# A conformer block on one core: the plan derived anew, with block order and PSUM banks searched together

## The chip, the cores and the metric

The kernel runs on one core of a Trainium2 chip. The metric is device time in microseconds (us) of one execution. The core has five instruction streams that run side by side and wait for each other by semaphores: PE (TensorE, the matmuls), ACT (ScalarE, activations), DVE (VectorE, elementwise work), POOL (GpSimd, small elementwise work) and SP (SyncE, which here only issues DMAs).

## The reference

Two sequences of 4000 tokens with 144 channels go through one conformer block. Cut to what is computed:

```
x = x + 0.5 * (silu(ln(x) @ w_ff1a) @ w_ff1b)          # 144 -> 576 -> 144
q, k, v = split(ln(x) @ w_qkv), 4 heads of 36
x = x + softmax(q k^T * 36**-0.5) v @ w_o               # 4000 x 4000 per head
a, b = split(ln(x) @ w_pw1);  h = a * sigmoid(b)
x = x + silu(depthwise_conv5(h)) @ w_pw2
x = x + 0.5 * (silu(ln(x) @ w_ff2a) @ w_ff2b)
return ln(x)
```

Inputs and output are bf16, x and the output have the shape (2, 4000, 144).

## The kernel before

**Tiling.** The 8000 tokens are 16 chunks of 500, eight for each sequence; a chunk is four blocks of 125 tokens, which lie on the partitions. X stays in SBUF. A chunk passes three stages. `pre` (L1267) is the first feed-forward (`ff1`, L1200) and then `pre2` (L1241), which makes the queries, keys and values. Attention runs over 18 phases: a phase is one chunk of queries against keys in tiles of 64 keys, 63 tiles in all (62 of 64 keys, one of 32). The first two chunks of queries have two phases each, since the last keys of the first sequence come late; their sums are saved between. `post1` (L1341) and `post2` (L1465) do the output projection, the gated convolution and the second feed-forward.

**An attention tile.** PE makes scores for 64 keys and 500 queries of four heads (two PSUM banks, four matmuls QK), ACT or DVE makes the exponentials, PE multiplies them with the values (four matmuls PV into banks 6 and 7). On ACT one instruction of 1000 columns does a tile (`emit_exp`, L1631). On DVE a tile takes five instructions (`dve_tile`, L1645): two that bring 500 columns each from PSUM to an integer, two that take the bits apart, and one product. Such a tile leaves two factors, so it has eight PV matmuls instead of four.

**Turning a chunk round.** Before a matmul of the feed-forward or of q, k, v the normalized chunk must have its channels on the partitions. For the very first chunk and at the end PE does it. Everywhere else it goes through DRAM (`blocks`, L885): DVE transposes blocks of 32 x 32, SP issues four DMAs that write the rows to a scratch tensor (`rows<-XN` or `rows<-AN`), waits until they have landed, and issues two DMAs that read them back: `XT<-rows` for the feed-forwards, the output projection and the gate, `XTQ<-rows` for q, k and v. SP works its list in order: a read that waits for its writes holds up all that stand behind it. Ahead of the DVE transpose stands the layer norm (`ln`, L953): statistics on DVE, then a power and four scalings on POOL.

**What sets the order.** While the program is built, `Rec.op` (L148) notes every instruction with the tiles that it reads and writes and a cost in us; `Rec.LAT`, `SEM` and `SWITCH` are added for latencies. Generators (`Thread`, `Sched`, L378 to L450) say what could go on, and `pick_any` (L1785) takes the next by estimated times and by the numbers in `POLICY` (L496), which hold for stretches of 21 attention tiles. In `blocks` a DMA of SP costs 0.36 us, a write lands 2.0 us and a read 2.4 us after it:

```
SP_COST = 0.36
W_LAT = 2.0
T_LAT = 2.4
```

All of this makes a first order, cut into blocks (what one step of a generator issued on one engine). `reorder` (L208) then moves the blocks of each engine by the table `ORDER` (L35): one letter for a block, P for one that stays, letters behind or ahead of it for one that moves by so many places. `finish` (L242) works out which semaphores each instruction must wait for, and `replay` (L286) issues the lists; nothing is decided on the chip. Since all is issued by line 296, every record of the profile has that line, and the names of the tiles tell what it is.

**PSUM.** Banks 0 to 5 are handed out by `Banks` (L326) as the first order is made. A tile keeps the bank that it was given there, whatever `reorder` does with its block, and the waits on a bank are those of the first order: an instruction that writes a bank waits for the readers of the tile that had it before.

**At the start and the end** there are dummy matmuls on the identity (`warm`, L781): 50 at first, and more wherever the first order shows a gap on PE before the first exponential and after the last.

Of the kernel before, what the change touches and what calls it, by code (L numbers as in the profile page):

```python
# [22 lines left out]
NB = 4  # L23
# [13 lines left out]
        "PPPPPPQOPPPPPQOPPPSPPMPPPQRNQNPPPQOROQNXOOOPPMOOhPggNPRILJLNRJOKLJNLMMMMMMPPPPPRPNPPPPQOPPRPNPPPPPPP"  # L37
        "PPPQOPPPQOUUNNNNNPPPWWNNOOLNNPPPQSPMOQOPQQNPP^PNOZZMOZKKLLLLMKRTMMPNPRPNPPPPQOPPPPPPPPPPPPPPQOPPPPPP"
        "SOOOWQVMRWSJKKQJNPPROOPPPPPPQOPPPPPPPPPPPQQNPPPPPQOPPPQOPQOPPPQOQOPRPNPSOOQNPQOPPSOOQNPPROOPQOPPQOPP"
        "WOPUMUVMMJLRSLSLUULTOUJUJTNTHSKRSTLTVFUKLSLSLLQNPPRRRMMQQNPPPPPPQOPQOPPQOQOQQQMPPSOOOPSPNOPPPQQNPPPQ"  # L40
        "QNPPQOPPQOPPQOPPRPNPPPPPPPPPQOPPPPPPQOPPPRRNNPPQOPPQQNQOPRRNQQQKPPPPPPPPPPRORPMPQOPPPPPQOQOPPQOQOQOP"
        "PPPPPQOPPPPPPPQQNPPPPPPPQOROOPPPPPQOPPPPPPPPQOQQNPPPPPPPPPPPPPPPPPSQRMMQQNPPPPQOPPQRNQQMPQOPPQOPPQOP"
        "PPPPPPPPPPPPPPPPPPPPPPPPPPPPPPPPQOQRRMQMPQQNROOQOPPQQQMPPPPQOPPPPPPPPQOPPPPPPPPPQOPQOPPPPQQNPPPPPPPP"
        "PPPPQOPPPPPPPPPPPPPPPPPPPPPPPPPQOTOQNSMPTMPNORPNPROQRMQQMPPPPQUNOSNNSMOQNPROOPRPQMSPNOPPSOPNQOPRPNPQ"
        "OQOPPQOTOPNOPPPPPQOPPPPPPPPPPPPPQOPPPQQNPPPSOOOPPPPQOQQNPQQRMQRRRKMPSQNNSOOQQMPPQQNQOPPPPSOOOPPQQQMP"
        "PPPPPPPQQNPPPQOPPQOPRPQMPPPPPQOPPTQNNOPPPPPPQQNPPSOOOPPQOPPPPPPPPPPPPPQOPRPNPQOPPQQNROOPQQNPPPPPPPPP"
        "PQOPPPPPPPPQOPPPPPPPPPPPPPQOPPQOPPPPPPPPPPPPPPPPPPPPPPPPSSOMQMPPQQNPQRNRNOQQQMPSOOOPPQQQQLPQOQOROOTP"
        "NOOPPPPPQOPPPPQOPPQOPQOPPPPPPPPPPQOPPPPQOPPQQNQOURNNNQNPPPPPRPQMPPPPPPPPRORNQQQLPSOOOQQQQQKPPQQNQOPP"
        "PPPPPQOPPPPPPPSOOOPPQOQOPPROOPQQN]OOOOOPNXNORLQLLQNPPROORRSNLVNWNNNNNOQNQOPQOPPPPPPPPPPPPPPPQOPPPPQO"
        "PROOPQQNPPPQQNPPPQOPPPPPPPQOPPPPQOPPPQQNPQOQOQOPPPQQNPPPQRNQNPPQOPPPPPPPPPPPPPROOPPPPPPPPPPPPQOPPPRO"  # L50
        "QNPQQNPQOROOPQOQQQQQKROOSOOQNPQOPPPPQOPQOPPPPPPPPPPPPPPQOPPPQOPPPPPPPQOPPQOPPWOOOOOOOQRPMPROOPPPPPPP"
        "PPQOQQNPQQQMQQQMQTPMRNNRPNPRPNPPPPPQQNRRRNLQQNPPQOPQOPSPNOTOOROMPPPRPNPQOSSSMMMQQNPPPQQNQOQQNQQQMQOP"
        "PPQQNPRRNNPPQRNOPPPPPQOPPSOOOPQQNRRNNPPPQQQQLPPPQOPPQQNROOTOOPNSOOOPPRTQMPQKPQQNPPRSQMMPPPPPPPPPPPPP"
        "PQOPPPPPPPPPPQOROOSOOQNQOPQQNPPPPPPQOPPPPQOPQOPPPPPTOPSMPQLPQOQOPQOPPQRPMSOPNSQNNPPPPPPPPPPPPPPQOPPP"
        "PPRRNNPQQNRPQRLOQRPMRRNNPRPNPRPNPQOPQRNOWOOPNOPNPPPSSNOMPQQNPPPPPQOPQOPPQOPQTNSNOSLOQNQOPPQOPPPQOPRP"
        "QMPPPQOPPPPQOPQOPQOPQOQOPRPNPPPPPQQQRLOPRPNPPPPPPPPPPPPPPPQOQOQOSOOOPPQOPPPPPQOQOPPPPPPPPPPQQQMPPPPP"
        "PPPPPQOPPPROQNPPPPPQOPPSOOOPSORNNPSOPNPPPPPPQOPPPPPPPPPPPPPPPPPPPPPPPPPPSOOOPPPPPPPPPPPPQOQOPPPPPQQV"
        "MRTQLRKQQIPPRPNQOPPPPQOQQNPPPROQNPPQOPPPPQQQMROOPQOPRSSMMQMQOQRRMQMQQNSQOTLPNQNQOQOQOPPQQNTQSMMQRLVN"
        "OOPNQNPPQQNPPPQQNROOQOPROOQOPQOPPPQOPPPPQOQOPPPPQOPQOPPPPPPPPQOPPPQOQOQQQMPPPUPNOOQQMRPNTOOOOPPQQNPS"
        "OOOQQNPPPPPPPQOPROTNOOOPQOPPPPPPPQOPPQOPPQOPQOPPQOPQQNQORRNNPPPQOPPQOPQOQOPPPPQSPMQNPPPPROQNPPPPPPPP"  # L60
        "PPPPPPPPPPQORRSMMOPSORNRMQNPPPQRNOPQRNOQOPPQOPPPPQOPPPPPPPROOPQOPQOPSOPQMPQQNPPPPPPPQOPPPPPPPPPPPPQO"
        "PPPQOPPPROQNROOPPPPPPPPQOPPPROOPPPPQOPQOPPQOPPPPPPQOPQOPPQOPPPQOPQOPQOQOPPPPPPPPPQOPPPPPPPPPPPQOPPPP"
        "PPPPPQQNPPQOPQQNPPPQOPPQOPPQOSOORROLPSPNQNPPPPPPPPPPPQOPPQOPPQOPPPPPPPPPPQOPPRPNQOPPPRPNVOOOOOOROQNP"
        "QQQQLPQORPNPQRNOROOPRORNOTOQRTQSSIISQKNPRPNPPPQOPPPPPPPTTOSLMMQQSMORPMQOTOPNQNPROOQOQOQQNQRRMQQRRJQM"
        "PPROQRPLQQQMQQNQSNPNPQQQQRKOTQXRLLPPKOOQOPSTNNNOPPPQOPQOPPRTNVMQNPPJQO"
    ),
    "act": (
        "PPPPPPPPPPPPPPQOROOPPQOPPQOQOPPPROOSOOOPQOQOPQOQOPPPPPPPPPPPPRPNPPPPPPPPROOPQOPPPPPPPPPPPPPPPPPPQOPP"
        "QOPPPPPPPPPPPPPPPPPPPPPPPPPPPPPPPPPPPPPPPPPPPPPPPPPPROOQOPPPPPPPPPPPPPPPPPPPPPPPPPPPPPPPPPPPPPPPPPPP"
        "PPPPPPPPPPPPPPPPPPPPPPPPPPPPPPPPPPPPPPPPPPPPPPPQOPPPPPPPPPPPPPPPPPPPPPPPPPPPPPPPPPPPPPPPPPPPPPPPPPPP"  # L70
        "PPPPPPPPPPPPPPPPPPPPPPPPPPPPPPPPPPPPPPPPPPPPPPPPPPPPPPPPPPPPPPQOPPPPPPPPPPPPPPPPPPPPPPQOPPPPPPPPPPPP"
        "PPPPPPPPPPPPPPPPQOPPPQOPQOPPPPPPPPPPPPPPPPPPPPPPPPPPPPPPPQQNPQOPPPPPPPPPPPPPPSOOOROOPPPPPPPPPPPPPPPP"
        "PPPPPPPPPPPPPPPPPPPPPPPPPPPPPPPPPPPPQOQOPPQOPPPPPPPPPPPPPPPPPPPPPPPPPPPPPPPPPPPPPPPQOPPPPPPPPPPPPPPP"
        "PPPPPPPPPPPPPPPPPPPPPPPPSOOOPQOPPPPPQOPPPPPPPPPPPPPPPPPPPPPPPPPPPPPPPPPPPQOPPPPPPPPPPPPPPPPPPPPPPPPP"
        "PPPPPPPPPPPPPPPPPPPPPPPPPPPPPPPPPPPPPPPPPPPPPPPPQOPPPPPPPPPPPPPPPPQOPPPPPQOPPPPPPPPPPPPPPPPPPPPPPPPP"
        "PPPPPQOPPPPPPPPPPPPPPPPPPPPQOPPPPPPQOQOPPPPPPPPQOPPPPPPPPPPPPPPPPPPPPROOPQOPPPPPPPPPPPPPPPPPPPPPPPPP"
        "PPPPPQOPPPPPPPPPPPPPPPPPPPPPPPPPQOPPPQOPPPPPPPPPPPPPPPPPPPPPPPPPPPPPPPPPPPPPPPPPPPPPPPPPPPPPPPQOPPPP"
        "PPPPPPPPPPPPPPPPPPQOPPPPPPPPPPPPPPPPPPPPPPPPPPPPPPPPPPPPPPPSOOOPPQOPPPPPPPPPPPPROQSSOKNVOOOOOO"
    ),
    "dve": (  # L80
        "PPROQQQLPPQORPNPQQRPLQOPPPQOTPTOOPRIRNOQSPPRPJQRNSNSSMRLRPQSIVNPPPPJPWRPNRKSMMOR^NNOOOOOOaNNNNNOOOOO"
        "OOPNPNPPPPPQOPPPPPPPPPPQOPPPPQOPQOPPPQQNROQQQLQORSNSMRMQQLPPQOPPPQQNPPQOPPPPPPQOQOPPPPRRRRRTQQTGQOEQ"
        "OSSURLSTJTMHNOSORNkMPQMPMOOOOOOOPPPPKOOPNOOOOPQOPPPPPPPQOPPPPPPQOPPPQOQOPPPPPPiPPMPPMPPPPQQQQLPEPPPL"
        "PNOPPPPPPPPPQOQOPPPPPPPPPPPPPPPPQOPPPPPPQQNROQQMQQQMPPQOPPPPPQOPPPPPPPPPPPQOPPPPPPPROQQMPPPPQOQOPPPP"
        "PPPPPPPPPPPPPPQOPPPPPPPPPPPPPQOPPPPPPPPQOPSPPMQOPQOPPQQQMPPPPPPPPQOROQSXPQRPRSTZQLRPQSP=RRR<QQQQGQOQ"
        "OPQOQRNQSQLSPSSNORPQQQQBPQOPPPPQOPPPPPQQNPQQNPPPPRPQQLPQOPPPPPPQOQQUPLPPMPPPPPPPPPQOQORPQQQKPPPPPPPP"
        "PPPPPPPPPPPPPPPPPPPPPPPPPPPPPPPROQNQOPQQNQOQOPPPPPROOPQQNPPPPROOPPPPPQOPPPPPPQOPROQRRTQQRHJQQQRPVQQN"
        "QOQQCQOPPQQNRPNQOQOQOQQNQQXPPKQNQMQMQOQQNPQOPPPPPPZPNOOPNPNPQMPQOPPPPPPPPPPPPP^OOPNOOPPMOOOdPMOOOOOO"
        "OOPNOOPNOOOPPPPQOPPPPQOPQQNPQOPROOPPQOPQOQOQQNPQOQOQOPQOQOPPPRTNNOOPPPPPPPPROQVSOOQNQRPQQRPQQQR=QRPL"
        "RPQSPKQRPQKPPPQOPPPQOQOPPPPPQOPPPPPPPPPPQOQOPPPPPPPQOPROSYOLNOOOOOOPPPPPWOOOOOOOPPPPPPPPPUOOOOOPPPPQ"  # L90
        "OPPPPROOPQQNPPQOQOQSNOOQQNPPPPPPPPQOQQNQQQQLQQNQOPPPPPPPPVOOOOPNPPPPPPPQOROOPPPPPQQNPPPQOPPQOROQNPPP"
        "PQOPPPPPPPPPPPPPPQQRPLPPPPPQOQOPPPPPQOPPTOOOOPPPPPPPPPPPPQOPPPPQOPPROOdOOPNOQOPPKOOOROMPMOPPPPPPPPQO"
        "PPPQOPPPQOPPSOOQNPPPPPPPPQOPPPPPPPPPPPPPRYQQLPKOOOOQQNPPQOPPPPPPPPPPPPPPPSORNQMPPQOPPQOPPPQOQOQQNQQN"
        "PPPPPQQUPLOOOPPPPPPPQOQOPROOQOPPPPQRNQNPPPSOVOPPPUOPPPEQQQMPPPQOPPPQOPPPPPPPPPQOQOQQNQQNQOPPPPPPPPPP"
        "PPPPPPPQOPPPPROOPQOPPQOPP[PPMOPPMPPPLPPZQNPPPPPQSNPEPPPPPPPPPRPRMQNPPPQOPPPPPPPPPPWPNPNPPWPPJOPNQNQO"
        "QOPPPPQOPPQQNQOPQOPQT]MPNPKOPPMOOOSPPMPPaOOSNNNNPNPNOOOOOPPQQQQLPPPPPPPPPQORROMPQOUOPPRLRPLZP]MNOMNO"
        "OOKOWNWMOMOOLRNOPSTPQXRJJUPLOLSMWOMOOOOO"
    ),
    "pool": (
        "PPPTOPNOPPPPPPPPPPQOPPPQQQQQQQIPPPPPQOZOOOOOOOPPWTKYMMTLSKNK[VKNNNNOQQKSPKOQOPPWPPPPQJNPPQOPUOOUSMMO"  # L100
        "LPQQQQLPPPPPPPPPQOPPQO"
    ),
    "sp": (
        "PPPPPPPQRTTLMNNPPPPPPPPPPRRNNPPRRNNPPPPPPRRNNPPPPPPRRNNPPPPPSORNNPPPPRRNNPQOPPPPPPPPPPVOOOOOOPPPPXXN"
        "NNNNNNNPWOOOOOOOPPVOOPNPNPPPPYOOOO]NNNNNOOOOOOQTPPPJ"
    ),
}


def c_pe(n):  # L110
    return n / 2400 + 0.0025

# [4 lines left out]

def c_act(n):
    return n / 1200 + 0.053


class Op:
    __slots__ = ("eng", "name", "a", "k", "idx", "deps", "clock", "inc", "waits", "cnt", "q", "done", "t0", "t1", "kind", "step")


class Rec:

# [18 lines left out]
    def op(self, eng, name, *a, r=(), w=(), q=None, cost=0.1, kind=None, lat=None, bub=(0.0, 0.0), **k):  # L148
# [4 lines left out]
        for key in r:  # L153
            h = self.hist.setdefault(key, ([], []))
            o.deps += [(d, True) for d in h[0]]
            h[1].append(o)
# [1818 lines left out]
```

## Time and profile before

| | before |
|---|---|
| time, median of 3 runs | 918.17 us (917.6 to 918.59) |
| the profiled execution's own time | 915.92 us |
| its span, first to last instruction | 914.1 us |
| busy: PE, ACT, DVE, POOL | 868.7, 859.5, 812.6, 294.7 us |
| mean granted clock of TensorE | 0.989 |
| exponentials on ACT (1000 columns) | 810, busy 757.3 us |
| exponential tiles on DVE | 182 |

The profiled execution is 2.25 us shorter than the median of the others, and 1.82 us of it lie outside the span. A busy time is the union of what an engine's instructions cover; the ends of matmuls are modelled, so PE counts as busy while it drains. "PE PS <- DMA XT<-rows" in the view of the waits means that PE was idle before a matmul and that the landing of this transfer ended the idle time. Times within the span are counted from its start.

### The profile page before, as it was taken

The page shows a single profiled execution, that of the slowest core. Times are in us where ns is not written, and L with a number is a line of the kernel's source. Part 1 is how long each engine was busy: PE and PEld are TensorE (multiplying, and loading weights), DVE is VectorE, ACT ScalarE, POOL GpSimd, SP SyncE. Part 2 cuts the span into 40 slices and gives each one's busy share as a digit, 9 for nine tenths or more (in the row PEclk, how much of TensorE's full clock was granted, in tenths as well). Part 3 has the DMA queues.
Part 4 walks back from the last instruction along what each step waited for, and adds up shares of the span by engine and source line. Part 5 has one row for each costly group of instructions (what it writes and reads, how often), then busy time and mean ns, then how long its engine had stood idle before and what let it go on. Part 6 is the DMA issues. An engine that isn't in the chain of part 4 may idle for free.

```text
span 914.1 us, 27059 instructions
## 1 busy us (share of the span) xinstructions
PE 868.7 (95%) x11493; PEld 391.2 (43%) x11493; DVE 812.6 (89%) x1774; ACT 859.5 (94%) x1099; POOL 294.7 (32%) x575
## 2 busy tenths in 40 slices
PE   8889999999999999999999999999998999999997
PEld 7434333434343333344435444443443344343466
DVE  8875889999999999999988979798786989899987
ACT  5779999999998999999999999999998999999974
POOL 7542131422153242033123505362234003073333
PEclk9989999999999999999999999999999999999999
DMA  4211101121102110112100020201001101000110
GB/s 108 67 42 36 36 9 36 29 43 29 29 13 59 30 32 12 29 30 42 23 22 22 17 47 16 55 22 29 22 22 37 27 15 29 16 22 21 24 34 27
DMA packets 114222, 28.81 MB, mean 32 GB/s; under 512 B 101085, under 2 KB 114100, under 8 KB 114100
## 3 DMA queue, kind: packets, MB, share of 16 engines
q1 hardware_dynamic: 112644, 26.46, 13.3%
q8 instruction: 90, 1.47, 0.7%
q10 hardware_dynamic: 1456, 0.62, 0.3%
q14 instruction: 32, 0.26, 0.1%
HBM read 13.44 MB, written 13.61 MB: 30 GB/s over the span
## 4 chain that ended last, share of the span: by engine, by line
PE 37%; ACT 26%; DVE 21%; DMA 7%; SPq 5%; POOL 2%; issue 1%; DVEq 0%; POOLq 0%
PE PS L296 37%; ACT PT L296 23%; DVE PT L296 11%; SPq L296 5%; ACT TH L296 3%; DMA rows<-XN 3%; DMA XT<-rows 2%; DVE ST L296 2%; DVE HT L296 2%; DVE X L296 2%; DVE XN L296 1%; POOL XN L296 1%; DMA XTQ<-rows 1%; DVE QT L296 1%; DMA rows<-AN 1%
## 5 line engine op out<-in xcount | busy, mean ns | idle before, releaser
L296 ACT ACTIVATE PT<-PS 128x1000 bf16<-128x1000 f32 (+1 forms) x826 | 765.1, 1052 | 12.8 <-PE PS L296 10.7
L296 PE MATMUL PS<-QT,KT 64*64 64x500 bf16 x3968 | 424.1, 386 | 15.2 <-ACT PT L296 8.7
L296 PE MATMUL PS<-PT,VA 64*37 64x500 bf16 x4696 | 413.8, 374 | 2.3 <-DVE QT L296 1.1
L296 DVE TENSOR_SCALAR PT<-PS 128x500 int16<-128x500 f32 x364 | 240.8, 669 | 12.1 <-PE PS L296 10.0
L296 PEld LDWEIGHTS PS<-QT,KT 64*64 64x64 bf16 x3968 | 124.7, 104 | 229.8 <-ACT PT L296 124.9
L296 POOL TENSOR_SCALAR RS<-ST 125x4 f32<-125x4 f32 x132 | 36.0, 273 | 528.2 <-DVE ST L296 521.6
L296 PEld LDWEIGHTS PS<-PT,VA 64*37 64x37 bf16 x4696 | 140.3, 96 | 102.1 <-DVE PT L296 19.0
L296 POOL TENSOR_SCALAR XN<-X,RS 125x144 bf16<-125x144 bf16 x264 | 150.9, 603 | 7.5 <-DMA out_dram<-XN 0.7
L296 DVE TENSOR_SCALAR PT<-PT 128x1000 uint16<-128x1000 uint16 x364 | 147.2, 416 | 2.9 <-PE PS L296 1.2
L296 DVE TENSOR_TENSOR PT<-PT 128x1000 bf16<-128x1000 bf16 x182 | 123.3, 679 | 1.3
L296 ACT ACTIVATE TH<-PS 128x500 bf16<-128x500 f32 (+3 forms) x194 | 104.5, 556 | 10.3 <-PE PS L296 9.7
L296 DVE SCALAR_TENSOR_TENSOR HT<-TH,PS 128x500 bf16<-128x500 bf16 (+1 forms) x135 | 81.6, 618 | 25.7 <-ACT TH L296 25.2
L296 POOL TENSOR_TENSOR RS<-RS,NHALF 125x4 f32<-125x4 f32 (+2 forms) x93 | 90.7, 977 | 38.8 <-DVE RS L296 33.2
L296 PE MATMUL PS<-XT,WA 128*128 128x500 bf16 (+4 forms) x288 | 76.7, 371 | 6.7 <-DMA XT<-rows 5.4
L296 DVE SCALAR_TENSOR_TENSOR X<-PS,X 125x288 bf16<-125x288 f32 (+1 forms) x128 | 57.5, 452 | 19.5 <-PE PS L296 18.3
L296 DVE BATCH_NORM_STATS2 ST<-X 125x6 f32<-125x288 bf16 x160 | 67.4, 459 | 0.3
L296 PE MATMUL PS<-WB,HT 128*125 128x144 bf16 (+1 forms) x640 | 52.5, 230 | 0.0
L296 PEld LDWEIGHTS PS<-WB,HT 128*125 128x125 bf16 (+1 forms) x640 | 44.5, 136 | 15.4 <-issue 5.4
L296 PEld LDWEIGHTS PS<-XT,WA 128*128 128x128 bf16 (+1 forms) x288 | 21.4, 99 | 39.6 <-issue 10.6
L296 PE MATMUL PS<-U,DG 128*128 128x250 bf16 (+5 forms) x204 | 29.4, 264 | 0.2 <-DVE PT L296 0.2
L296 DVE STREAM_TRANSPOSE XN<-XN 128x320 f32<-128x320 f32 x54 | 27.0, 500 | 0.6 <-POOL XN L296 0.6
L296 DVE CAST KT<-PS 128x500 bf16<-128x500 f32 (+1 forms) x29 | 19.0, 654 | 8.0 <-PE PS L296 7.9
(95 smaller groups left out, 525.4 us busy)
## 6 DMA issues: line engine op xcount, KB each, us to landing
rows<-XN SPq DMA_DIRECT2D x216, 40.0 KB, 2.0
XT<-rows SPq DMA_DIRECT2D x56, 128.0 KB, 2.0
rows<-AN SPq DMA_DIRECT2D x60, 40.0 KB, 2.0
X<-in_x_dram SPq DMA_DIRECT2D x16, 140.6 KB
XTQ<-rows SPq DMA_DIRECT2D x26, 70.3 KB
out_dram<-XN SPq DMA_DIRECT2D x13, 140.6 KB
XT<-rows SPq DMA_DIRECT2D x56, 16.0 KB, 1.9
out_dram<-XN SPq DMA_DIRECT2D x4, 70.3 KB
```

Of the source, the lines that this page charges most:

```text
L296: ins = getattr(eng, o.name)(*o.a, **o.k)
```

## The change

The costs that the plan is made with are set anew, and the plan is derived from them. In `blocks` a write costs SP 0.615 us and lands 1.31 us after it; the two reads have costs of their own (0.43 and 0.36 us for `XT`, 0.815 us for each `XTQ`) and land 1.4 us (1.7 us for `XTQ`) after. Some costs of PE, ACT and POOL change by 0.009 to 0.7 us. All tables of `POLICY` and `ORDER` are new. In addition the bank of each PSUM tile is read from a table, `PLACES`, one digit for each of the 1722 tiles in the order in which they are taken; `Place` remembers the slot of the first order beside the bank. `reorder` drops the dependences that came from sharing a slot and makes new ones from the new order of PE: the first matmul of a tile waits for the readers of the tiles that had its banks before. The arithmetic, the number of buffers and the DMAs' shapes are the same.

```diff
 ORDER = {
     "pe": (
-        "PPPPPPQOPPPPPQOPPPSPPMPPPQRNQNPPPQOROQNXOOOPPMOOhPggNPRILJLNRJOKLJNLMMMMMMPPPPPRPNPPPPQOPPRPNPPPPPPP"
+        "PPPPPPPPPPPPPPPQRPMQYZMNXMNLMOPKKTOOOOPQRPMROOQOPPQ`ROO]]IMQOLOQHILLMPPQOQOPPPPUOTNNNQMSSNRMMROOPROQ"
...
+PLACES = (
+    "4521053402453140531342402305054232142034202403253421500201420412040212045534025405240524032543250313"
...
+    def place(self, slot, n):
+        no, at = len(self.tiles), int(PLACES[len(self.tiles)])
+        self.tiles.append(tuple(range(at, at + n)))
+        out = []
+        for j in range(n):
+            p = Place(at + j)
+            p.slot, p.no = slot + j, no
+            out.append(p)
+        return tuple(out)
...
     def reorder(self, table):
...
+        users = {}
+        for o in self.ops:
+            drop = o.shared - o.own
+            o.deps = [(d, raw) for d, raw in o.deps if id(d) not in drop]
+            if o.tile is not None and o.eng != "pe":
+                users.setdefault(o.tile, []).append(o)
+        last, prior = {}, {}
+        for o in lines["pe"]:
+            k = o.tile
+            if k is None:
+                continue
+            if k not in prior:
+                prior[k] = {last[b] for b in self.tiles[k] if b in last}
+                last.update({b: k for b in self.tiles[k]})
+            for p in prior[k]:
+                o.deps += [(d, False) for d in users[p]]
...
     def spawn(self, gens):
-        me, ready = self.cur, max(self.cur.ready, self.R.last if self.stepped else 0.0)
+        me, n0 = self.cur, self.n0
+        ready = max([self.cur.ready] + [o.done for o in self.R.ops[n0:]])
...
-    SP_COST = 0.36
-    W_LAT = 2.0
-    T_LAT = 2.4
+    W_COST, W_LAT = 0.615, 1.31
+    T_LAT = 1.4
...
-                [(XTQF[0:HD, k, cc, :, :], HD * k, HD * k + HD, TB) for k in range(2)], f"tq{cc}", wk)
+                [(XTQF[0:HD, k, cc, :, :], HD * k, HD * k + HD, TB, 0.815, 1.7) for k in range(2)], f"tq{cc}", wk)
...
-    XN_COST = 0.45
+    XN_COST = 0.53
     XN_LAT = 0.6
-    XN_FIRST = 0.8
+    XN_FIRST = 0.1
...
```

`W_COST`, `cost` and `lat` stand where `SP_COST`, `W_LAT` and `T_LAT` stood in `blocks`; the rest of the diff is numbers of `POLICY` and small additions to costs.

## The prediction

> **What bounds the kernel now.** I read the page's busy line first, then the chain that ended last, then the windows by stage, then the waits that a DMA ended.
>
> ```profile
> PE 868.7 (95%) x11493; PEld 391.2 (43%) x11493; DVE 812.6 (89%) x1774; ACT 859.5 (94%) x1099; POOL 294.7 (32%) x575
> PE 37%; ACT 26%; DVE 21%; DMA 7%; SPq 5%; POOL 2%; issue 1%; DVEq 0%; POOLq 0%
> ```
>
> Three engines are nearly full, and the chain changes between them. 12% of it are DMAs and their issue on SP, which belong to the chunks turned round through DRAM.
>
> ```profile
> 0.00:92.00 92.00, 81.13 (x954) 46.46 (x954) 68.94 (x174) 68.73 (x111) 46.69 (x99) 0.94 0.27 63
> 92.00:165.00 73.00, 69.51 (x932) 26.94 (x926) 64.69 (x143) 71.17 (x84) 18.17 (x35) 1.00 0.14 29
> 165.00:878.00 713.00, 688.05 (x9244) 291.48 (x9242) 651.01 (x1359) 700.05 (x860) 216.71 (x418) 1.00 0.13 28
> 878.00:914.00 36.00, 30.04 (x375) 26.36 (x371) 27.99 (x101) 19.58 (x47) 13.10 (x25) 0.95 0.08 23
> 60.00:80.00 20.00, 16.91 (x174) 7.39 (x173) 9.68 (x19) 14.32 (x23) 3.34 (x7) 0.83 0.21 45
> 64.00:70.00 6.00, 5.79 (x54) 2.70 (x56) 2.15 (x5) 2.58 (x5) 0.00 (x0) 0.50 0.05 15
> ```
>
> The columns after the length are busy us of PE, PEld, DVE, ACT and POOL, then the granted clock. 165 is the end of the first four phases, 878 of the last. In the middle ACT has 13.0 us idle of 713: that is all that a better order can win there. ACT's other idle time is 25.1 us before 165 and 16.4 us after 878. In 60 to 80 all engines are slack and the clock is 0.83.
>
> ```profile
> 54.90 5.76 SPq L296 DMA_DIRECT2D rows<-XN  x8
> 60.71 1.73 SPq L296 DMA_DIRECT2D XTQ<-rows  x2
> 62.48 0.98 SPq L296 DMA_DIRECT2D XT<-rows  x2
> 69.29 2.60 SPq L296 DMA_DIRECT2D rows<-XN  x4
> 74.24 1.67 SPq L296 DMA_DIRECT2D XTQ<-rows  x2
> ```
>
> SP's list shows why. Four writes take 2.6 to 2.9 us of SP (the plan before: 1.44), the read can leave 1.4 us after the last (at 514.7 after 510.73 + 2.55), and two `XTQ` reads take 1.67 us (plan: 0.72). At 54.90 two chunks' writes stand together: the first four would have ended at 57.8 and their read left at 59.2; it left at 60.71, behind the other four.
>
> ```profile
> 34.19 0.63 PE L296 MATMUL PS<-XT,WA 128*128 128x500 bf16 x2 [2.95 <-DMA XT<-rows]
> 39.84 0.40 PE L296 MATMUL PS<-XT,WA 128*128 128x500 bf16 x1 [0.65 <-DMA XT<-rows]
> ...
> 64.20 1.85 PE L296 MATMUL PS<-XTQ,WK 72*128 72x500 bf16 x4 [2.61 <-DMA XTQ<-rows]
> ...
> 101.61 1.02 PE L296 MATMUL PS<-XTQ,WK 72*128 72x500 bf16 x4 [1.06 <-DMA XTQ<-rows]
> ```
> ```profile
> PE PS L296 <- DMA XT<-rows: 8.7, 7, 3.0
> PE PS L296 <- DMA XTQ<-rows: 6.0, 6, 2.6
> ```
>
> PE stood idle for DMAs 14.7 us. Before 165 it was 2.95 + 0.65 for `XT` and 2.61 + 0.30 + 1.06 for `XTQ`, 7.6 together; 7.1 come later.
>
> **The change, part by part.**
>
> *Work.* The new costs, the new `spawn` and `POLICY` act only through the order; none is executed. Counted in the order of instructions, there are 6 tiles more on DVE and 6 fewer exponentials on ACT. ACT: 6 x 757.3/810 = -5.6, but 13 copies more (8 of `XT` at 0.375, five at 0.3 to 0.6) and five tanh for silu: +5.9, so ACT +0.3. DVE: a tile is 2 x 240.8/364 + 2 x 147.2/364 + 123.3/182 = 2.8, six 16.8; five more products for tanh +3.0; copies left to ACT -5.0: +14.8. PE: 24 PV at 413.8/4696 = +2.1, and 34 dummies at 15.3/187 = +2.8, which fill gaps at the start and the end. Changes between kinds of matmul fall from 816 to 781; those that leave attention (15 fewer) start 0.30 us after the last matmul where a group of four takes 0.21, so -1.4. PE is thus even where it counts. In the first four phases DVE gets 6.6 us more (131.3 to 137.9, priced from start to start), and DVE has 31.4 us idle there. This costs between 0 (all beside other work) and 6.6; I take +2.0, since DVE is 88% full in that stretch once it is shorter.
>
> *XT in the front.* For each chunk I sum the matmuls that stand in PE's list between the last one the chunk's layer norm needs and the first one that reads the landed chunk, each at its mean distance to the next start (0.06 to 0.07 for QK and PV, 0.075 for `HT,WB`, 0.27 for 500 columns of feed-forward). This cover was 14.7 and 19.5 for the two that stalled, where 17.3 and 22.5 us passed. Now it is 25.5 and 34.5. Both stalls go: -3.6. What is late next is `XTQ`.
>
> *XTQ in the front.* The five covers were 19.2, 14.1, 16.5, 17.9, 19.5, and 21.6, 19.9, 18.0, 19.5, 20.0 us passed. Now they are 15.8, 14.9, 15.1, 17.0, 20.1. That is shorter, but SP's list there no longer has two chunks' writes together: four writes, their reads, the next four. What does such a chunk need? The second ran 58.15 (residual) to 63.4 (POOL's last scaling); its DVE transpose came only at 68.76, behind copies that waited in DVE's list for the stalled K projection. From SP's first write at 69.29 to the matmul at 77.62 are 8.3. Without the wait that is 57.7 to 72.4: 14.7, the lower bound. The upper is the 19.5 that ended a stall. I take 16.1, at which the sixth chunk, alone on SP, passed without a stall. Shortfalls: 0.3 + 1.2 + 1.0 = 2.5 for 4.0 before: -1.5 (bounds -4.0 and +11.2).
>
> *The clock.* From 63.8 to 70.5 it is at half or little more: 20 us x 0.17 = 3.4 us of PE. It followed the 2.61 us stall, and elsewhere a stall of 0.90 (at 282) and one of 1.92 (at 695), 1.7 us each, but not the 2.95 at 31 nor 0.92, 0.96 and 1.06. So a stall of about 1 us has one chance in four or five. Of the 3.4 I leave 1.0 for the new stalls: -2.4 (bounds 0 and -3.4). [...]
>
> *The middle, 165 to 878.* Covers of the seven `XTQ` chunks were 16.0 to 28.0 and are 15.3 to 31.4, of the shortest `XT` after attention 7.3 and 8.9, now 8.9 and 9.2, where about 10 is needed. So 1.92 and about 1.5 more of stalls go, with the drop of 1.7 after the former; three pairs of chunks stand together on SP where there was one, for which I count 1.5 (what it cost the read at 60.71). Of 5.1 minus 1.5, half reaches the end, because ACT works ahead: -1.8 (bounds +3 and -7). The waits on banks are as before: 527 exponentials find the bank's last reader two places back on ACT, where 526 did, so banks are costed at nothing; the cover is the exponential between. ACT's list has two waits for stores of the output more, where a buffer of the last layer norms is used again; behind them stand that norm's scalings alone, after the last phase, and the store was issued more than 20 matmuls ahead: nothing.
>
> *The end.* 20 real matmuls fewer stand after the last phase, and 22 more dummies. The chain there is one chunk's latency: -0.5 (0 to -3).
>
> Sum: +2.0 - 3.6 - 1.5 - 2.4 - 1.8 - 0.5 = -7.8. Against the profiled execution's 915.92 that is 908.1; the median of the runs shown lies 2.25 above it, so 918.17 - 7.8 = **910.4 us**.
>
> **The rivals.**
>
> *XTQ takes the place of XT (slower).* If a chunk needs 19.0 and not 16.1, the four short covers fail by 3.2 + 4.1 + 3.9 + 2.0 = 13.2 against 4.0 before, and the clock gains nothing: +9.2 + 2.0 - 3.6 - 1.8 - 0.5 = +5.3, 923.5 us. It decides from a need of about 18 on: the shortfalls are four times the need less 62.8, and they must outweigh the 4.0 of before and the other terms, -3.9 without and -6.3 with the clock, which is at 17.7 and 18.3. For it: three of five passages were 19.5 or more. Against it: those had another chunk's DMAs or a stalled DVE list before them, and later ones passed in 16.1 to 17.6.
>
> *All of it works (faster still).* At a need of 14.7, with the DVE tiles hidden and 4 us won in the middle: -3.6 - 4.0 - 2.4 - 4.0 - 0.5 = -14.5, 903.7 us. For it: ACT has 13 us idle in the middle. Against it: POOL and DVE queue differently now, and the DVE has 14.8 us more.
>
> *The change buys nothing.* The stalls go, but ACT waits for DVE instead, whose 6.6 us more lie all in the front: -9.8 + 6.6 + 3 of new stalls in the middle = about 0, 918 us. DVE's 31.4 us idle in the front speak against it.
>
> **How the numbers follow.** Forecast 0.52 (its own range 906 to 915), all works 0.20, nothing 0.07, slower 0.21. The predicted time is the forecast's, 910.4. The range 902 to 921 leaves out about 0.08 below and 0.10 of the slower case above. A difference under 0.2% (1.8 us) can't be told from none here: faster 0.72, same 0.07, slower 0.21.
>
> **What would show it.** The profile after should show no idle time over 1 us before `XT,WA` between 25 and 60; SP never with eight writes in a row before 150; the clock of 1.00 from 20 to 160; PE's waits for `XT` and `XTQ` below 10 us together; the end of the fourth phase near 158; ACT's idle time in the middle at 11 us. Waits for `XTQ` of 2 us or more before 110, with the clock at half behind them, would mean the slower rival. DVE over 95% busy before 160 while ACT waits would mean that the tiles cost more than 2.0.

## The result and the profile after

The changed kernel takes 902.8 us, the median of four executions (901.42 to 905.37); the kernel before took 918.18 beside it (917.6 to 918.59). The ratio is 0.9836, with a 95% interval of 0.9814 to 0.9859. Run again on another chip it took 901.83 (900.46 to 905.25) where the kernel before took 914.11 (910.37 to 916.64): 0.9872, 0.9847 to 0.9896. The kernel before varies more: 910.37 to 919.79 in the 55 executions taken beside the experiments, with medians of 912.45 to 915.6, against 900.46 to 905.37 in ten of the new one, with medians of 902.8 and 901.83; the change is worth 12 to 15 us.

The profiled execution of the changed kernel took 902.71 us, its span is 900.9, its mean granted clock 0.999. First the busy line and the chain that ended last, of the page of after:

```profile
PE 859.1 (95%) x11551; PEld 390.2 (43%) x11551; DVE 822.6 (91%) x1796; ACT 856.2 (95%) x1106; POOL 296.1 (33%) x575
ACT 50%; PE 23%; DVE 15%; DMA 6%; SPq 3%; issue 1%; POOL 1%; POOLq 0%; DVEq 0%
```

PE has 58 matmuls more and is busy 9.6 us less. Half of the chain now runs over ACT (26% before), a quarter over PE (37% before). Then the windows by stage, with the same columns as before (length; busy us of PE, PEld, DVE, ACT, POOL; clock; share of the DMA engines; GB/s). The first four phases now end at 155, the last at 867, so that three lines answer to 0 to 165, 165 to 878 and 878 to the end; the last two lines are the stretches that were shown of before.

```profile
0.00:155.00 155.00, 144.59 (x1905) 72.45 (x1906) 138.06 (x327) 136.52 (x196) 63.47 (x130) 1.00 0.22 50
155.00:867.00 712.00, 686.69 (x9276) 291.95 (x9274) 657.60 (x1375) 700.63 (x863) 221.89 (x431) 1.00 0.13 29
867.00:900.90 33.90, 27.84 (x371) 25.76 (x371) 26.92 (x96) 19.09 (x48) 10.71 (x15) 0.98 0.06 18
...
60.00:80.00 20.00, 19.16 (x233) 9.87 (x235) 14.58 (x32) 17.86 (x29) 10.03 (x21) 1.00 0.22 46
64.00:70.00 6.00, 5.35 (x82) 3.10 (x81) 4.66 (x12) 4.41 (x8) 3.01 (x8) 1.00 0.21 45
```

The stretch from 60 to 80, slack before on every engine and at a clock of 0.83, is dense and at full clock: 17.86 us of ACT's work in it instead of 14.32. By the end of each phase's last PV matmul, 10.3 us are won in the first four phases, 1.6 in the other fourteen, 1.3 after the last: 13.2 in all, the difference of the spans. Much of it is clock: at mean granted clocks of 0.989 and 0.999 the two profiled executions lost 10.1 and 0.9 us of it, so, counted one for one, 9.2 of the 13.2; over all executions it is less, as the third experiment shows. SP's list in the front, in which eight writes stood in a row before:

```profile
42.11 3.73 SPq L365 DMA_DIRECT2D rows<-XN  x4
47.25 0.82 SPq L365 DMA_DIRECT2D XT<-rows  x2
48.12 2.55 SPq L365 DMA_DIRECT2D rows<-XN  x4
52.08 1.31 SPq L365 DMA_DIRECT2D XT<-rows  x2
53.44 2.55 SPq L365 DMA_DIRECT2D rows<-XN  x4
57.40 0.82 SPq L365 DMA_DIRECT2D XT<-rows  x2
58.26 2.55 SPq L365 DMA_DIRECT2D rows<-XN  x4
62.21 1.72 SPq L365 DMA_DIRECT2D XTQ<-rows  x2
66.55 3.11 SPq L365 DMA_DIRECT2D rows<-XN  x4
71.06 1.67 SPq L365 DMA_DIRECT2D XTQ<-rows  x2
```

Each chunk's four writes are followed by their own reads, to 150. PE's stalls on transfers in the front (idle time ahead of the matmul in brackets):

```profile
35.16 0.63 PE L365 MATMUL PS<-XT,WA 128*128 128x500 bf16 x2 [1.11 <-DMA XT<-rows]
...
65.67 1.02 PE L365 MATMUL PS<-XTQ,WK 72*128 72x500 bf16 x4 [0.65 <-DMA XTQ<-rows]
```

They are all of these that are left there: 1.76 us, where there were 7.6. But over the whole span the view of PE's waits gives (us, times, longest; `PT` are exponentials, `HT` the hidden layer of a feed-forward):

```profile
PE PS L365 <- DMA XT<-rows: 11.2, 12, 1.8
PE PS L365 <- ACT PT L365: 7.2, 22, 0.8
...
PE PS L365 <- DVE PT L365: 1.8, 7, 0.3
...
PE PS L365 <- DMA XTQ<-rows: 1.3, 2, 0.7
PE PS L365 <- DVE HT L365: 1.2, 5, 0.4
```

The waits for `XT` have grown, from 8.7 to 11.2: behind the first four phases they went from 5.1 to 10.1. The gain is bought in the front, and it is larger than the stalls that went there.

### The profile page after: what moved, and what is told of

Read it like the earlier page. It is cut to its first block, busy times and chain, and to the rows that moved or that the text cites. A ratio compares the mean times of both kernels' runs of the same rounds, so it can differ in the third digit from the quotient of the medians.

```text
span 900.9 us, 27264 instructions
## 1 busy us (share of the span) xinstructions
PE 859.1 (95%) x11551; PEld 390.2 (43%) x11551; DVE 822.6 (91%) x1796; ACT 856.2 (95%) x1106; POOL 296.1 (33%) x575
## 4 chain that ended last, share of the span: by engine, by line
ACT 50%; PE 23%; DVE 15%; DMA 6%; SPq 3%; issue 1%; POOL 1%; POOLq 0%; DVEq 0%
ACT PT L365 45%; PE PS L365 23%; DVE PT L365 7%; ACT TH L365 5%; SPq L365 3%; DMA rows<-XN 3%; DMA XT<-rows 2%; DVE HT L365 1%; DVE X L365 1%; DVE XN L365 1%; DVE ST L365 1%; DVE QT L365 1%; DVE KT L365 1%; DVE AN L365 1%; DMA XTQ<-rows 1%
## 5 line engine op out<-in xcount | busy, mean ns | idle before, releaser
L365 ACT ACTIVATE PT<-PS 128x1000 bf16<-128x1000 f32 (+1 forms) x820 | 757.1, 1062 | 5.3 <-PE PS L365 3.8
L365 PE MATMUL PS<-QT,KT 64*64 64x500 bf16 x3968 | 420.3, 385 | 13.6 <-ACT PT L365 7.0
L365 PE MATMUL PS<-PT,VA 64*37 64x500 bf16 x4720 | 405.4, 372 | 2.3 <-DVE QT L365 0.8
L365 DVE TENSOR_SCALAR PT<-PS 128x500 int16<-128x500 f32 x376 | 247.7, 667 | 13.1 <-PE PS L365 11.1
L365 DVE TENSOR_SCALAR PT<-PT 128x1000 uint16<-128x1000 uint16 x376 | 151.2, 417 | 1.4
L365 DVE TENSOR_TENSOR PT<-PT 128x1000 bf16<-128x1000 bf16 x188 | 126.2, 674 | 1.0
L365 DVE SCALAR_TENSOR_TENSOR HT<-TH,PS 128x500 bf16<-128x500 bf16 (+1 forms) x140 | 84.4, 616 | 20.2 <-ACT TH L365 18.7
L365 PE MATMUL PS<-XT,WA 128*128 128x500 bf16 (+5 forms) x288 | 75.9, 365 | 8.7 <-DMA XT<-rows 7.5
L365 DVE BATCH_NORM_STATS2 ST<-X 125x6 f32<-125x288 bf16 (+1 forms) x160 | 65.6, 446 | 0.3
L365 PEld LDWEIGHTS PS<-XT,WA 128*128 128x128 bf16 (+1 forms) x288 | 20.6, 97 | 40.9 <-DMA XT<-rows 10.5
L365 POOL COPY U<-U 128x2 bf16<-128x2 bf16 (+1 forms) x54 | 11.6, 255 | 57.4 <-DVE U L365 57.4
```

What stands on the lines that cost most here:

```text
L365: ins = getattr(eng, o.name)(*o.a, **o.k)
```

## The experiments

Four questions: does the gain come from the stalls on SP's transfers and the half clock behind them (theory A) or from the whole plan (theory B); what do the new costs with their `POLICY`, and what does the search, bring; what are the searched banks worth; and what do the stalls cost that are left.

### One read moved ahead on SP, in the kernel before

```diff
+        sp = lines["sp"]
+        i = next(n for n, o in enumerate(sp) if o.q == "d8") + 4
...
+        lines["sp"] = sp[:i] + sp[i + 4:i + 6] + sp[i:i + 4] + sp[i + 6:]
```

In `reorder`, the pair `XTQ<-rows` of the eight-writes place moves ahead of the second chunk's four writes.

> The kernel before, with one change in SP's list: the read of the first XTQ chunk (tq3) is put ahead of the four writes of the XT chunk (d1) that stood before it. Theory A (the gain comes from SP's list in the front and the half clock behind its stalls): the read leaves 1.5 us earlier, the stall before the K projection at 64 falls from 2.6 to about 1.1 us, the clock stays at 1.00 between 60 and 72, and the time falls by 1.5 + 3.4 = 4.9 at most, 913 to 915.5 us. Theory B (the gain is spread over the whole plan: banks and order searched together): the front's stalls are made up by ACT's backlog later, 917 to 918.5 us.

Measured: 916.11 us (914.54 to 918.64), the kernel before 915.41; ratio 1.0004, 0.9982 to 1.0026. SP's list and the stalls of this run:

```profile
55.97 3.66 SPq L300 DMA_DIRECT2D rows<-XN  x4
61.04 1.74 SPq L300 DMA_DIRECT2D XTQ<-rows  x2
62.82 2.59 SPq L300 DMA_DIRECT2D rows<-XN  x4
66.83 0.81 SPq L300 DMA_DIRECT2D XT<-rows  x2
```
```profile
64.48 1.12 PE L300 MATMUL PS<-XTQ,WK 72*128 72x500 bf16 x4 [1.81 <-DMA XTQ<-rows]
69.08 1.01 PE L300 MATMUL PS<-XT,WA 128*128 128x500 bf16 x2 [1.54 <-DMA XT<-rows]
...
104.16 1.02 PE L300 MATMUL PS<-XTQ,WK 72*128 72x500 bf16 x4 [1.80 <-DMA XTQ<-rows]
```

The read is first in line and still leaves at 61.04 (60.71 before): the four writes alone took 3.66 us of SP here, where eight had taken 5.76, and they started 1.1 later. The stall shrank by 0.8, the chunk that was moved back stalled for 1.54 in its place, and a later one for 1.80 (1.06 before, at 101.61). The clock fell too: it is 0.56 from 64 to 75. One place on SP is not the cause; theory A fails in this form.

### The stall filled with dummy matmuls, in the kernel before

```diff
+NDUMMY = 64
...
+        pe = lines["pe"]
+        i = next(n for n, o in enumerate(pe) if any(d.q == "tq3" for d, raw in o.deps))
+        lines["pe"] = pe[:i] + [self.dummy() for _ in range(NDUMMY)] + pe[i:]
...
```

A dummy is a matmul of the identity on 12 columns of bank 7 that nothing else uses.

> The kernel before, with 64 dummy matmuls of 12 columns (unused columns of bank 7) right ahead of the K projection that stalls at 64 us; nothing else moves, SP's list neither. The landing still ends the wait, so what was idle is now filled. Theory A: the clock stays at 1.00 behind the wait, 3.4 us of PE are won, 914.5 to 916 us; if the dummies last longer than the 2.6 us of the wait, that much is lost again. Theory B: 917.5 to 919 us.

Measured: 917.38 us (913.58 to 923.1); ratio 1.0029, 1.0004 to 1.0055. The dummies and the stalled matmuls, and the window behind:

```profile
62.02 1.76 PE L308 MATMUL PS<-IDENT 128*128 128x12 bf16 x64
65.22 1.85 PE L308 MATMUL PS<-XTQ,WK 72*128 72x500 bf16 x4 [1.44 <-DMA XTQ<-rows]
```
```profile
64.00:71.00 7.00, 5.78 (x54) 2.70 (x56) 2.13 (x5) 2.57 (x5) 0.00 (x0) 0.53 0.12 34
```

The clock fell all the same, to 0.53 from 64 to 71, so the run does not separate the clock from the stall. Here 1.76 us of such narrow matmuls, with 1.44 us of idle time behind them, did not keep it up.

### The price of the clock, from the executions themselves

Each execution comes with its span and mean granted clock; (1 - clock) x span is the clock time that it lost. In 55 executions of the kernel before, taken beside the experiments on three chips, that is 9.4 us in the mean (clock 0.984 to 0.995), and a straight line through them is 905.3 us + 1.02 x the loss, with a correlation of 0.87. In the ten executions of the changed kernel it is 3.2 us, and the line is 899.5 + 0.96 x the loss, with a correlation of 0.67. So a microsecond of lost clock goes with about a microsecond of time in both. This is rough: in the four variants here with ten executions each, the slope lies between 0.47 and 1.02. Of the 12.3 us between the means (914.9 and 902.6), 6.1 are clock that is no longer lost, and 5.9 remain at a full clock. The lines are correlations; no run here parts the stalls of the kernel before from its drops, so that fewer stalls made the drops fewer is argued, not shown. The last section has what the profiles say for it.

### The first orders, without the search

```diff
-ORDER = {
...
-}
+ORDER = dict(pe="", act="", dve="", pool="", sp="")
...
-        no, at = len(self.tiles), int(PLACES[len(self.tiles)])
+        no, at = len(self.tiles), slot
```

The second part stands only in the changed kernel, where it gives each tile the bank of its slot. Of the kernel before:

> The kernel before with every block at the place and every tile in the bank that its planner first gave it (no moved blocks). Theory P (the plan: the new DMA times and the POLICY found with them carry the gain, the search of the order adds the same to both kernels): slower than the kernel before by as much as the changed kernel's first order is slower than the changed kernel, 15 to 30 us, so 933 to 948. Theory S (the search: order and banks sought together win more than the order alone did): also slower than the kernel before, but by less than the changed kernel's first order loses, 10 to 15 us, so 928 to 933.

Of the changed kernel:

> The changed kernel's own first order: new DMA times, new POLICY, no moved blocks, every tile in the bank that the planner gave it. Theory P: about 15 us below the first order of the kernel before, so 918 to 933. Theory S: within 5 us of the first order of the kernel before, so that the whole gain of 15 comes out of the search.

Measured on one chip: 927.56 us (923.28 to 930.31) for the first order of before and 914.11 (912.52 to 919.77) for that of after, beside 912.45 for the kernel before; ratios 1.0161 (1.0115 to 1.0207) and 1.0021 (0.9994 to 1.0049). The new first order is 13.4 us better than the old one, near the 15 of theory P, though both times came out below the ranges that P gave (933 to 948 and 918 to 933). The search took 15.1 us off the old, and 12.3 off the new if its second series (901.83, below) is set beside it, 13.6 by the ratios. At equal clock the step is smaller: 914.11 has 2.8 us of lost clock in the mean, 927.56 has 10.9, so 8 of the 13.4 are clock. If the lost clock is taken off each mean, one for one, the search is worth about 11 us to the old and 13 to the new. Which of the two it helped more is therefore open. Where in the span, by the start of the instruction on DVE that saves a phase's sums, in the four profiles:

| | first four phases | the rest | span |
|---|---|---|---|
| before, first order | 167.0 | 756.0 | 923.0 |
| before | 165.6 | 748.5 | 914.1 |
| after, first order | 162.3 | 748.4 | 910.7 |
| after | 155.6 | 745.3 | 900.9 |

The new costs and `POLICY` (with the new `spawn`, which no run takes apart) win 4.7 us in the front and 7.6 behind it. The search over order alone had won 1.4 in the front; that over order and banks won 6.7 there. The clock is 1.00 in the front of both of the latter profiles; PE is idle 2.1 us less (12.5 and 10.4), and 4.6 us less busy for almost as many matmuls (1916 and 1910). How the order packs them closer is not taken apart here.

The DMA times apart from `POLICY`: the old times put into the new first order, and by the reverse edit the new times into the old one. The reads' own costs and landing times go with them.

```diff
-    W_COST, W_LAT = 0.615, 1.31
-    T_LAT = 1.4
+    W_COST, W_LAT = 0.36, 2.0
+    T_LAT = 2.4
...
```

> The same first order of the changed kernel, with the DMA times of the kernel before put back (0.36 an issue, 2.0 and 2.4 to land) and all else new. If the DMA times are what the first order gains by: 5 to 12 us slower than the first order with the new times, with eight writes in a row on SP again and more than 10 us of PE's waits for XT and XTQ. If not (theory S, or the other costs and POLICY): within 3 us of it.

> The first order of the kernel before, with its own POLICY, but the DMA times of the changed kernel (0.615 and 1.31 for a write, 0.36 to 0.815 and 1.4 to 1.7 for a read). Theory T (true DMA times make the better first order whatever the POLICY): 4 to 13 us below the first order of the kernel before, 915 to 923, and PE's waits for XT and XTQ below 8 us instead of 12.3. Theory F (the numbers of POLICY are fitted to the costs that they were found with, so that any mixture of old and new loses): 8 to 30 us above it, 935 to 957.

And a control, the new times off by 0.05 us:

```diff
-    W_COST, W_LAT = 0.615, 1.31
-    T_LAT = 1.4
+    W_COST, W_LAT = 0.615, 1.36
+    T_LAT = 1.45
```

> The first order of the changed kernel with its DMA latencies off by only 0.05 us (1.36 and 1.45 instead of 1.31 and 1.4). Theory T: as near the truth as before, so within 4 us of 914. Theory F: the plan goes another way at the first choice that tips, and the numbers of POLICY, which hold for stretches of the plan, no longer fit: 922 or more.

Measured:

| first order with | `POLICY` and other costs of before | `POLICY` and other costs of after |
|---|---|---|
| DMA times of before | 927.56 | 946.09 (945.88 to 947.69) |
| DMA times of after | 949.09 (948.46 to 952.21) | 914.11 |
| times of after + 0.05 us | not run | 930.65 (930.34 to 931.41) |

PE's waits in the first order of before, and in the same with the new DMA times:

```profile
PE PS L224 <- ACT PT L224: 7.8, 23, 1.0
PE PS L224 <- DMA XT<-rows: 6.9, 5, 2.5
PE PS L224 <- DMA XTQ<-rows: 5.4, 5, 2.5
```
```profile
PE PS L224 <- DMA XT<-rows: 19.1, 15, 3.0
PE PS L224 <- ACT PT L224: 14.7, 40, 0.9
...
PE PS L224 <- DMA XTQ<-rows: 1.6, 2, 1.1
```

The new DMA times alone, which are nearer to the 2.55 to 3.31 us that four writes take on SP in the front of the profile of before, make the plan 21.5 us worse (21.3 by the ratios, 1.0394 and 1.0161), and its waits for `XT` grow to 19.1. The old times in the new plan cost 32.0 us, where 5 to 12 or under 3 had been expected; SP has eight writes in a row there again (at 27.84, 48.97 and 134.43). Theory T falls, theory F stands: times that are off by only 0.05 us cost 15 us by the ratios (1.0183 and 1.0021), 16.5 by the times. That run agrees with the other to 162.3 at the end of the fourth phase; it loses its time later, with ACT's waits for scores at 15.2 us instead of 7.9. The likely reason, which no run shows by itself, is that the numbers of `POLICY` hold for stretches of a plan, and once a choice tips they meet other work. What the change brings is neither the times nor the numbers but the pair.

### Other banks under the same order

`PLACES` filled by a plain rule in place of the search (among the free banks, the one whose last reader can be done first), 1313 of 1722 tiles in other banks:

> The changed kernel, with the order of every engine as it is and the table of PSUM banks replaced by a plain rule: each tile takes, in PE's order, the free banks whose last readers could be done first (1313 of 1722 tiles get other banks; the last 60 matmuls ahead of the end and the end keep theirs). Theory A: banks are worth nothing beside the order, 901 to 905 us, PE's waits for ACT's and DVE's reading of PSUM within 3 us of those with the table. Theory B: without the searched banks the exponentials wait, 908 to 918 us.

Measured: 933.96 us (932.55 to 935.17); ratio to before 1.0217, 1.0192 to 1.0242. That is 31 us above the changed kernel with not one instruction moved. Both theories had too little (905 and 918 at most).

The slots of the first order as banks, save four tiles; 208 change their bank:

```diff
-        no, at = len(self.tiles), int(PLACES[len(self.tiles)])
+        no = len(self.tiles)
+        at = {24: 2, 164: 1, 705: 0, 914: 1}.get(no, slot)
```

> The changed kernel with its order untouched, each PSUM tile in the bank that the planner first gave it, save four that the order forbids; 208 of 1722 tiles change their bank. If the searched banks are worth nothing of themselves (the prediction's term): 901 to 905, as the changed kernel. If sought banks carry part of the gain (theory S): 907 to 918, with PE's wait for PT by ACT above the 7.2 us that it has now.

Measured: 938.07 us (935.89 to 941.79); ratio to before 1.0285, 1.0247 to 1.0322; 35 us above the changed kernel, where theory S had 918 at most. PE's waits in this run:

```profile
PE PS L366 <- ACT PT L366: 13.9, 33, 1.2
PE PS L366 <- DVE PT L366: 9.7, 21, 1.5
PE PS L366 <- DMA XT<-rows: 6.7, 9, 1.8
PE PS L366 <- DVE HT L366: 5.3, 8, 1.4
PE PS L366 <- DVE X L366: 4.7, 10, 0.6
```

Against the same lines of after: 7.2 for `PT` by ACT, 1.8 for `PT` by DVE, 1.2 for `HT`, and under 0.3 for `X`. Apart from the transfers, nearly all of them are matmuls that write a bank that an instruction of DVE or ACT has yet to read. ACT's list, which is the same in both kernels, runs 19.9 us late at 160, 35 at 860 and 39 at its last instruction.

I then counted, with the times of the changed kernel's own profile, how many tiles would find their bank's last reader still at work when their first matmul starts, and by how much:

| banks | tiles too early | sum, us | of it before 160 | measured loss | of it in the front |
|---|---|---|---|---|---|
| searched | 0 | 0 | 0 | 0 | 0 |
| slots of the first order | 92 | 45.5 | 19.5 | 35 | 20 |
| plain rule | 163 | 56.5 | 11.0 | 31 | 7 |
| slots in the front only | 35 | 18.8 | 18.8 | 19 | 20 |

The losses have clock in them: the mean execution loses 10.5, 1.9 and 8.6 us of it in these three runs, in the order of the table, and 3.2 in the changed kernel. Without that, one for one, they are about 29, 33 and 13, which rank as the sums do.

The last row was worked out before its run, which puts back only the tiles of the first four phases:

```diff
-        no, at = len(self.tiles), int(PLACES[len(self.tiles)])
+        no = len(self.tiles)
+        at = slot if no < 276 and no not in (24, 164) else int(PLACES[no])
```

> The changed kernel, order untouched; only the tiles of the first four phases (the first 276 but two) go back to the bank of the first order, 75 of them another one than now. By the times of the changed kernel's profile 35 of these tiles would find their bank's last reader still at work when their first matmul starts, by 18.8 us in sum. Theory K (the order of the front can stand only on its own banks, and what is lost there stays lost): the fourth phase ends 17 to 21 us later than 155.6, and the time is 918 to 924. Rival: PE, 95% busy but rarely alone on the path, has the slack to make it up behind the front, so that less than 8 us reach the end: below 911.

Measured: 921.57 us (918.4 to 923.45); ratio to before 1.0058, 1.0039 to 1.0077. The fourth phase ends at 175.2, 19.6 late, and the fifth and sixth 19.9 and 20.4 late: what is lost in the front stays lost. The searched order of the front can't stand on the old banks. That does not say what the search would have reached with the banks held fast; the search is not in the source, and this stays open.

### The stalls that are left

Seven `XT` stalls in the middle are covered: the scores of one or two tiles go ahead of the stalled matmuls on PE, their exponentials ahead of the tanh on ACT.

```diff
+MOVES = (
...
+    ("pe", 3459, 3452),
+    ("pe", 3476, 3452),
+    ("act", 3475, 3467),
+    ("act", 3487, 3467),
...
+        for e, step, ahead in MOVES:
+            blk = [o for o in lines[e] if o.step == step]
+            rest = [o for o in lines[e] if o.step != step]
+            i = next(n for n, o in enumerate(rest) if o.step == ahead)
+            lines[e] = rest[:i] + blk + rest[i:]
```

The changed kernel as it is, for comparison:

> The changed kernel once more, on the chip of the next run, for comparison: 902 to 905, 0.982 to 0.986 of the kernel before.

With the moves:

> The changed kernel with seven of its XT stalls in the middle covered: there the scores of one or two tiles go ahead of the stalled matmuls on PE, and their exponentials ahead of the tanh on ACT. ACT is idle 0.64, 1.64, 0.63, 1.13, 0.84, 0.59 and about 0.5 us at these places, 6.0 together. Theory M (an XT stall in the middle costs what ACT is idle behind it, and that reaches the end): 4 to 6 us faster than the changed kernel, 897 to 900, with PE's wait for XT at 2 to 4 us. Theory W (the other waits take its place; ACT and the DMAs of the next chunk only meet later): within 1.5 us of the changed kernel.

Measured: 901.83 us for the changed kernel, just outside what was expected, and 901.86 (901.28 to 902.76) with the moves; ratios to before 0.9872 and 0.9868 (0.9846 to 0.9889). PE's waits of the changed kernel in this run, then with the moves:

```profile
PE PS L365 <- DMA XT<-rows: 8.6, 12, 1.4
PE PS L365 <- ACT PT L365: 7.2, 22, 0.8
```
```profile
PE PS L389 <- ACT PT L389: 9.1, 25, 0.8
PE PS L389 <- DMA XT<-rows: 3.6, 8, 1.0
```

The stalls went, 5.0 us of them, and nothing came of it. ACT has 692.1 us of work in 165 to 866 instead of 691.4, of 701. Where a stall went, PE waited a little later for a bank that an exponential held, and ACT for the tanh that had been moved back (0.95 us at 293.9). So theory W stands and M falls: these stalls were no longer on the path. No version here beats the changed kernel.

## Why the prediction was right and where it was off

*Direction, range.* 902.8 is faster, as forecast, and in the range of 902 to 921, near its lower end. The forecast itself was 910.4: it had -7.8 where -15.4 came on the first chip and -12.3 over all executions. It is also outside the forecast's own range of 906 to 915: the wide range held it, not the sum. The front was the right place to look (10.3 of the 13.2 us of the profiled pair came there), but its four terms add up to -5.5. The nearest rival was "all of it works", 903.7, with a chance of 0.20; its DVE tiles at nothing and most of its `XTQ` term came true (3.3 of 4.0), its 4 us in the middle did not.

*XT and XTQ in the front.* -3.6 and -1.5 were forecast. `XT` fell from 3.60 to 1.11, -2.5; `XTQ` from 3.97 to 0.65, -3.3. Together -5.8 for -5.1. The covers pointed the right way, and the need of 16.1 that was taken was too high: covers of 14.9 to 17.0 passed with one stall of 0.65. From the last matmul that these four chunks need to the first that reads them, 15.2, 15.1, 15.9 and 16.6 us passed. PE's whole idle time in the front fell by less than its stalls on transfers, by 4.0 (14.4 to 10.4), as other waits grew. That eight writes in a row held up the read was wrong in part: moved ahead, it left no earlier.

*The clock.* -2.4 was forecast, from one drop of 3.4 us with 1.0 left for new stalls. This is the term that was furthest off. In the profiled pair the front lost 165 x 0.03 = 5.0 us of clock before and none after; over all executions and the whole span the loss falls by 6.1. Two things were missing. The kernel before loses 9.4 us in the mean execution, in more places than the profiled one showed at 64 (its two variants above had drops elsewhere too: a clock of 0.64 from 34 to 36 and 0.56 from 106 to 108 in the first, 0.68 from 34 to 39 in the second). And 1.0 was left for new stalls, where the profile after shows no drop between 20 and 898.

The chance of one in four or five, by the length of a stall, was a poor measure too. In the profile of before the clock is 0.50 for 3.41 us from 9.08, 282.15 and 695.16 and for 6.83 us from 63.69. The matmuls behind the stalls of 2.61, 0.90 and 1.92 us start at 64.20, 281.51 and 695.31, each within 0.7 us of the start of one of these stretches. The longest stall, 2.95 us before 34.19, cost no clock, and neither did those of 1.06, 0.96 and 0.93. What decides between them was not shown.

The start shows the price of one drop. Changed kernel, 5 to 15 us, in the profile of the first chip and then in that of the second:

```profile
5.00:15.00 10.00, 6.94 (x97) 6.25 (x94) 9.38 (x35) 6.17 (x13) 7.40 (x17) 1.00 0.47 124
```
```profile
5.00:15.00 10.00, 7.25 (x77) 6.56 (x75) 9.12 (x34) 5.28 (x12) 7.42 (x17) 0.83 0.52 138
```

The second lost 1.7 us of clock there, and its phases ended 1.1 to 1.2 us later from the first to the tenth.

*The DVE tiles.* +2.0 was forecast between 0 and 6.6. DVE is busy 4.4 us more in the front (133.6 to 138.1) and its idle time there fell from 31.4 to about 17 us; the front ended 10 us earlier. No cost of these tiles shows, which fits the lower bound; none was measured apart.

*Work.* ACT is busy 3.3 us less (859.5 to 856.2) where 0.3 more was counted, as its exponentials take 8.0 less and not 5.6; DVE is busy 10.0 more where 14.8 was counted. Neither changes the account.

*The middle.* -1.8 was forecast and -1.6 came, ACT's idle time fell from 13.0 to 11.4 as said (11). The way there was wrong. The stalls on `XT` did not shrink but doubled in this profile, and the price put on them, half of a stall, was too high: five us of them taken away were worth nothing.

*The banks.* They were costed at nothing, because 527 exponentials find their bank's last reader two places back on ACT, where 526 did. For the table that was made this holds: PE's waits for `PT` by ACT are 7.2 us after 9.0. As a measure it was blind: the slots of the first order have 524 such exponentials, and only four with a reader one place back, and cost 35 us. What counts is the time by which a bank's last reader is done, on DVE as much as on ACT. That the banks let the order of the front close up (6.7 us won by the search there, where 1.4 had been) was in no term. It overlaps with the stalls and the clock above, so the two accounts of the front are not to be added.

*The end.* -0.5 was forecast, -1.3 came; the bounds were 0 and -3.

*What was to be seen.* Eight writes in a row: gone, as said. The clock of 1.00 from 20 to 160: as said. The end of the fourth phase near 158: 155. One stall of 1.11 before `XT,WA` at 35 where none over 1 was to be, and 12.5 us of waits for `XT` and `XTQ` where less than 10 was to be: wrong, and of no weight in the middle, as the last experiment shows.

## What to carry to other kernels

A plan made by a tuned scheduler is a pair of costs and tuning: truer costs under old tuning were worse by 21 us here, an error of 0.05 us by 15, so a new plan is judged as a whole and from the profile of the whole. When an order and its buffers are chosen together, price the buffers by time: for each first writer, how long the last reader of its bank will still be at work; the sums of this were 45.5, 56.5 and 18.8 us for measured losses of 35, 31 and 19 (about 29, 33 and 13 without the clock), where counting places showed nothing. And before a stall is priced, look at what is full beside it: 5 us of PE's stalls were free where ACT was busy 98% of the time, while in the slack front 5.8 us of stalls less came with 5.0 us of clock less lost.

## What the runs showed of the hardware

The same kernel in the same order loses between 4.5 and 14.7 us of TensorE's clock in the 55 executions (clock 0.995 to 0.984, spans 908.7 to 918), and its time follows with a slope of 1.02; a single profile gives only one draw of it.

In the profile of before the granted clock is 0.50 in four stretches that begin between 9 and 880 us, three of 3.41 us and one of 6.83, and 1.00 between them; in that of after it is 1.00 from 5.24 to 899.53. Between 20 and 890 us PE was idle for 0.90 us or more at a stretch seven times before (up to 2.95, 11.3 us in sum), and half clock began within 0.7 us of the end of three of these, of 2.61, 1.92 and 0.90 us. After, it was eight times (0.95 to 1.77, 9.8 us in sum), and the clock stayed at 1.00. So the length of a stall alone did not tell whether clock went with it: 0.90 us had half clock beside it, 1.77 and 2.95 had none. That no stall over 1.77 us is left in that profile, and no drop falls there, speaks for the step from fewer long stalls to fewer drops and does not prove it.

In the run with dummies, 64 matmuls of 12 columns took 1.76 us from 62.02, 1.44 us of idle time followed, and the clock was 0.53 from 64 to 71.

In the changed kernel's profile the issue of four writes on SP took 2.55 us at 48.12, 53.44 and 58.26, 3.73 at 42.11 and 3.11 at 66.55. The cost of 0.615 us for each write that the new plan counts with (2.46 for four) is near the shortest of these.
